# One list schedule for all engines' orders, and PSUM banks held in common, in an attention and MoE kernel

## The chip, the cores and the metric

The kernel runs on one core of a Trainium2 chip. The metric is the device time of one execution in microseconds (us). Five engines matter here: TensorE (PE, with its weight loads on a row of their own, PEld), VectorE (DVE), ScalarE (ACT), GpSimd (POOL) and SyncE (SP), which issues every DMA of this kernel. Each engine runs its own instructions strictly in the order in which the program holds them; an instruction that waits for a semaphore holds up everything behind it on its engine.

## The reference

Attention over 8 batches of 8 heads (576 positions, head size 64), in which scores more than tau below the maximum of their row are masked out. Its result goes through a two-layer block with a gated activation.

```python
scores = scale * np.matmul(q, k.transpose(0, 1, 3, 2))
thresh = np.max(scores, axis=-1, keepdims=True) - tau
scores = np.where(scores >= thresh, scores, -1000000000.0)
scores = scores - np.max(scores, axis=-1, keepdims=True)
attn = np.exp(scores)
attn = attn / (np.sum(attn, axis=-1, keepdims=True) + 1e-09)
out = np.matmul(attn, v)
...
h = x @ w_in                       # x: 4608 x 512, w_in: 512 x 2048
g = h * (1.0 / (1.0 + np.exp(-h)))
return (g @ w_out)                 # w_out: 2048 x 512
```

## The kernel before

**Attention.** The work goes by visits, one for a pair of heads, and by score tiles of 128 rows by 576 columns. A visit of batches 1 to 7 has nine tiles: four of each head, and one that holds the last 64 rows of both. Batch 0 is cut in two: four "low" visits with the first 256 rows, which take another path (transposes on PE), then four "high" visits with the other 320 rows. A tile goes through this chain. `scores` (L411): PE multiplies, with the keys split into a high and a low part; four matmuls of 288 columns, eight in the tile shared by two heads. `soft1`: DVE takes the row maximum (L421) and the threshold (L424). `soft1b`: ACT takes the exponential (L431). `soft2`: DVE masks and sums (L440), and takes the reciprocal (L444, L448). `soft2b`: ACT divides (L453). `soft3`: POOL makes a high part in half precision (L464; for the first tiles ACT does, L462) and two low parts (L467, L470), and SP issues a DMA that transposes them into `wT` (L480). After the last tile of a visit, `av` multiplies by the values (28 matmuls, L495), for two halves of the columns in batches 1 to 7; `av_post` splits the result into a high and a low part, `x16` (L513 on ACT, L514 on DVE). Two PSUM tiles hold scores, `x16` has two buffers, so that two batches can be under way.

**MoE.** When the last `av` of a batch half is through, that half gives 32 units: 16 of `h_unit` (12 matmuls, L529; then tanh on ACT L537, a product on DVE L538, the high part on ACT L546 and the low part on DVE L552, into `gbuf`), and 16 of `o_unit` (12 matmuls each, L567; four to an output tile, which ACT scales, L576, and SP stores, L578). There are 512 units in all, 64 to a batch.

**Preparing.** Queries and keys are loaded for each head (L290, L291) and split (L314, L315, L323, L325). The values are loaded for each pair (`vraw`, L232), their maximum is taken (L238), and a power of two for the batch (`vscale`, L110 to L136) scales their split (L275, L276). The 32 chunks of the weights come as 64-bit words and are decoded in the first part of the run by POOL, DVE, ACT and PE (L178 to L204), and split after that (L210, L211).

**What sets the order.** The program is written tile by tile: at step t come the softmax pieces of tile t, the scores of tile t+1, the last pieces of tile t-1, and what `at` planned for t; a `credit`, filled at a rate worked out for each batch half, says how many MoE units follow. Out of that the framework's scheduler, which runs a model of the engines, makes the order of each engine; `pri` raises chosen pieces by an offset (`PRI_S`, `PRI_SOFT1`, `PRI_SOFT2`). Of the eight PSUM banks four belong to the two score tiles, one to `av` (`ps_a`), and two, later three (`turn`), to everything else, taken in turn.

Of the kernel before, what the change touches and what calls it, by code (L numbers as in the profile page):

```python
# [19 lines left out]
P = 128  # L20
# [19 lines left out]
PRI_S, PRI_SOFT1, PRI_SOFT2 = 500, 50, 200  # L40

# [10 lines left out]
def attention_moe(  # L52
# [32 lines left out]

# [8 lines left out]


# [9 lines left out]
    def pow2_scales(mx, name, across=True):  # L105


        k = name[0]
        one = const.tile([P, 1], F32, name=f"{name}_one", tag=f"{k}_one")
        nc.vector.tensor_reduce(out=one, in_=mx, op=ALU.max, axis=AX.X)  # L110
        if across:


            diag = const.tile([P, P], BF16, name=f"{name}_diag", tag="diag")
            nc.scalar.activation(diag, ident, AF.Copy, scale=one)
            allp = bank([P, P], f"{name}_ps")
            nc.tensor.matmul(allp, ones, diag, start=True, stop=True)
            one = const.tile([P, 1], F32, name=f"{name}_all", tag=f"{k}_all")
            nc.vector.tensor_reduce(out=one, in_=allp, op=ALU.max, axis=AX.X)
        cl = const.tile([P, 1], F32, name=f"{name}_cl", tag=f"{k}_cl")  # L120
        nc.vector.tensor_scalar(
            out=cl, in0=one, scalar1=2.0**-20, scalar2=2.0**47, op0=ALU.max, op1=ALU.min
        )
        e2 = const.tile([P, 2], I32, name=f"{name}_e2", tag=f"{k}_e2")
        nc.vector.tensor_scalar(
            out=e2[:, 0:1], in0=cl.bitcast(I32), scalar1=EXPMASK, scalar2=None, op0=ALU.bitwise_and
        )
        nc.vector.tensor_scalar(
            out=e2[:, 1:2], in0=cl.bitcast(I32), scalar1=EXPMASK, scalar2=EXPMASK,
            op0=ALU.bitwise_and, op1=ALU.bitwise_xor,  # L130
        )
        sc = const.tile([P, 2], F32, name=f"{name}_sc", tag=f"{k}_sc", bufs=3)
        nc.vector.tensor_scalar(
            out=sc[:, 0:1], in0=e2[:, 1:2].bitcast(F32), scalar1=2.0**12, scalar2=None, op0=ALU.mult
        )
        nc.vector.tensor_scalar(  # L136
            out=sc[:, 1:2], in0=e2[:, 0:1].bitcast(F32), scalar1=2.0**-13, scalar2=None, op0=ALU.mult
        )
        return sc
# [6 lines left out]
    ones = const.tile([P, P], BF16, name="ones")  # L146
    nc.vector.memset(ones, 1.0)
    ident = const.tile([P, P], F32, name="ident")
    make_identity(nc, ident)
    wsc = {}  # L150

    w_words = (w_in.bitcast(I32), w_out.bitcast(I32))
    wraw = {}
    wps = {}

    def load_weights(i):
        if i < 4 * NK and i % 8 < 4:
# [12 lines left out]

    def decode_weights(i):


        t = wraw.pop(i)
        low, top = t[:, :, 0], t[:, :, 1]
        w = wst[:, i + WSPARE, :]
        wbits = w.bitcast(I32)
        nc.gpsimd.tensor_scalar(  # L178
            out=w, in0=top.bitcast(F32), scalar1=2.0**-112, scalar2=1.0,
            op0=ALU.mult, op1=ALU.mult,  # L180
        )
        nc.vector.tensor_scalar(
            out=wbits, in0=wbits, scalar1=3, scalar2=None, op0=ALU.logical_shift_left
        )
        nc.vector.scalar_tensor_tensor(  # L185
            out=wbits, in0=low, scalar=29, in1=wbits,
            op0=ALU.logical_shift_right, op1=ALU.bitwise_or,
        )


        n, c = divmod(i, 4)
        if c == 0:
            wps[n] = bank([P, P], f"wps_{n}", 2)
        upper = w.bitcast(BF16).rearrange("p (c t) -> p c t", t=2)[:, :, 1]
        for j in range(4):
            nc.tensor.matmul(
# [589 lines left out]
```

## Time and profile before

| what | value |
|---|---|
| timed runs | 1278.84, 1283.26, 1284.72 us; median 1283.26 us |
| span of the profiled execution | 1282.6 us; no other time of this execution is listed |
| TensorE clock granted, mean | 0.974 |
| instructions | 26842 |
| PE busy | 1164.2 us, 91% |
| DVE busy | 1001.3 us, 78% |
| ACT busy | 819.3 us, 64% |
| POOL busy | 794.6 us, 62% |
| DMA, packets' time as a share of 16 engines | 58.8%, 158.15 MB |

The page of the profile gives the busy time of each engine, then the span in 40 slices, then the DMA queues, the chain of work that ended last, and the groups of instructions by line. Other views of the trace give the same by stretches of time (busy time, granted clock and DMA share in each), by group with the idle time ahead of it, by who waited for whom, or instruction by instruction. A row of the groups reads: line, engine, operation, output and input, shape, count, then busy time in us and mean length of one in ns, then the idle time ahead of them and what ended it. The times of the three runs and the span agree within 0.3%.

### The profile page before, as it was taken

The page shows a single profiled execution, that of the slowest core. Times are in us where ns is not written, and L with a number is a line of the kernel's source. Part 1 is how long each engine was busy: PE and PEld are TensorE (multiplying, and loading weights), DVE is VectorE, ACT ScalarE, POOL GpSimd, SP SyncE. Part 2 cuts the span into 40 slices and gives each one's busy share as a digit, 9 for nine tenths or more (in the row PEclk, how much of TensorE's full clock was granted, in tenths as well). Part 3 has the DMA queues.
Part 4 walks back from the last instruction along what each step waited for, and adds up shares of the span by engine and source line. Part 5 has one row for each costly group of instructions (what it writes and reads, how often), then busy time and mean ns, then how long its engine had stood idle before and what let it go on. Part 6 is the DMA issues. An engine that isn't in the chain of part 4 may idle for free.

```text
span 1282.6 us, 26842 instructions
## 1 busy us (share of the span) xinstructions
PE 1164.2 (91%) x9400; PEld 891.7 (70%) x9400; DVE 1001.3 (78%) x2627; ACT 819.3 (64%) x1501; POOL 794.6 (62%) x956
## 2 busy tenths in 40 slices
PE   5675778799699989999999999999899999999998
PEld 3454546576577767777777777777677777877777
DVE  7999998987898978869795978868795979771431
ACT  5887767675777756757575757666575757661431
POOL 4559978676778657767665666776575766761000
PEclk8987899899999989999999999999999999999999
DMA  9456767868868557656755665657566655543000
GB/s 294 129 176 166 184 121 134 151 122 155 152 126 162 105 132 135 122 117 130 148 107 122 114 151 120 126 112 147 118 110 117 121 117 109 100 84 57 6 15 19
DMA packets 363479, 158.15 MB, mean 123 GB/s; under 512 B 329552, under 2 KB 338256, under 8 KB 363344
## 3 DMA queue, kind: packets, MB, share of 16 engines
q1 hardware_dynamic: 363344, 156.43, 58.8%
q8 instruction: 74, 1.21, 0.4%
q14 instruction: 61, 0.50, 0.1%
HBM read 66.72 MB, written 9.44 MB: 59 GB/s over the span
## 4 chain that ended last, share of the span: by engine, by line
PE 45%; DVE 26%; issue 8%; POOL 8%; DMA 7%; ACT 5%; SPq 1%; POOLq 0%; ACTq 0%; DVEq 0%
PE o L567 18%; PE h L529 14%; PE s L411 7%; PE a L495 6%; DVE w L440 5%; DVE sm L421 4%; DVE gbuf L552 4%; DMA wT<-hl 3%; POOL hl L467 3%; DVE qstack L315 2%; DMA vraw<-in_vL 2%; POOL hl L464 2%; DVE th L538 2%; POOL hl L470 2%; DVE wst L185 1%
## 5 line engine op out<-in xcount | busy, mean ns | idle before, releaser
L529 PE MATMUL h<-x,wst 128*128 128x288 f16 (+2 forms) x3072 | 417.2, 289 | 18.0 <-DVE th L538 16.3
L567 PE MATMUL o<-gbuf,wst 128*128 128x288 f16 (+2 forms) x3072 | 403.2, 287 | 8.2 <-DVE wst L211 5.8
L464 POOL TENSOR_SCALAR hl<-w 128x576 f16<-128x576 f32 x264 | 186.3, 706 | 294.1 <-ACT w L453 76.8
L529 PEld LDWEIGHTS <-wst 128*128 128x128 f16 x3072 | 290.5, 99 | 111.8 <-issue 31.2
L567 PEld LDWEIGHTS <-wst 128*128 128x128 f16 x3072 | 289.5, 98 | 95.4 <-DVE wst L211 9.2
L467 POOL TENSOR_TENSOR hl<-w,hl 128x512 f16<-128x512 f32 x272 | 338.3, 1244 | 12.4
L453 ACT ACTIVATE w<-w,sm 128x576 f32<-128x576 f32 x288 | 216.3, 769 | 109.4 <-DVE sm L448 103.6
L431 ACT ACTIVATE w<-s,sm 128x576 f32<-128x576 f32 x288 | 209.4, 735 | 117.6 <-POOL hl L470 74.8
L440 DVE SCALAR_TENSOR_TENSOR w<-s,sm,w 128x576 f32<-128x576 f32 x288 | 231.6, 811 | 64.8 <-ACT w L431 62.5
L421 DVE TENSOR_REDUCE sm<-s 128x1 f32<-128x576 f32 x288 | 214.7, 748 | 46.8 <-PE s L411 42.5
L411 PE MATMUL s<-khi,qstack 128*128 128x288 f32 x608 | 157.9, 342 | 42.6 <-DVE w L440 27.7
L552 DVE SCALAR_TENSOR_TENSOR gbuf<-th,gbuf 128x288 f16<-128x288 f32 (+2 forms) x256 | 158.6, 622 | 22.8 <-ACT gbuf L546 22.0
L495 PE MATMUL a<-wT,v 128*64 128x288 f16 (+1 forms) x1680 | 147.9, 302 | 8.4 <-DMA wT<-hl 6.8
L537 ACT ACTIVATE th<-h,msc 128x288 f32<-128x288 f32 (+2 forms) x256 | 126.1, 495 | 41.0 <-DVE gbuf L552 24.5
L411 PEld LDWEIGHTS s<-khi,qstack 128*128 128x128 f32 x608 | 96.1, 194 | 69.9 <-issue 52.0
L546 ACT ACTIVATE gbuf<-th 128x288 f16<-128x288 f32 (+2 forms) x252 | 110.0, 439 | 53.2 <-DVE th L538 52.7
L538 DVE SCALAR_TENSOR_TENSOR th<-th,h 128x288 f32<-128x288 f32 (+2 forms) x256 | 113.4, 445 | 30.7 <-ACT th L537 28.3
L411 PE MATMUL s<-klo,qstack 128*128 128x288 f32 x608 | 131.9, 299 | 0.0
L495 PEld LDWEIGHTS <-v 128*64 128x64 f16 x1680 | 94.7, 114 | 50.2 <-issue 39.5
L470 POOL TENSOR_TENSOR hl<-w,hl 128x64 f16<-128x64 f32 x272 | 122.0, 449 | 0.0
L325 POOL TENSOR_TENSOR klo<-kraw,khi 128x576 fp32r<-128x576 f32 x64 | 94.8, 1481 | 10.6 <-ACT khi L323 9.2
L411 PEld LDWEIGHTS s<-klo,qstack 128*128 128x128 f32 x608 | 99.9, 193 | 0.0
(85 smaller groups left out, 871.5 us busy)
## 6 DMA issues: line engine op xcount, KB each, us to landing
qraw<-in_qT SPq DMA_DIRECT2D x128, 144.0 KB, 3.0
kraw<-in_kT SPq DMA_DIRECT2D x128, 144.0 KB, 3.0
vraw<-in_vL SPq DMA_DIRECT2D x32, 320.0 KB, 3.6
wraw<-in_w_out SPq DMA_DIRECT2D x16, 512.0 KB, 3.9
out_t<-ot SPq DMA_DIRECT2D x56, 144.0 KB, 2.1
wT<-hl SPq DMA_TRANSPOSE x304, 3.3
gbuf<-in_w_in SPq DMA_DIRECT2D x8, 512.0 KB, 8.3
wraw<-in_w_in SPq DMA_DIRECT2D x8, 512.0 KB, 5.4
```

Source lines behind the costliest of these rows:

```text
L411: nc.tensor.matmul(s_ps[:, j, :HALF], lhs, kk[:, j * HALF : (j + 1) * HALF], start=(n == 0), stop=(n == len(seq) - 1),)
L421: nc.vector.tensor_reduce(out=negm, in_=s_ps[:, :, :HALF], op=ALU.max, axis=AX.XY, negate=True)
L431: nc.scalar.activation(wtile[t].rearrange("p (j c) -> p j c", j=2), sps[t][:, :, :HALF], AF.Exp, bias=small[t][:, 0:1],)
L440: nc.vector.scalar_tensor_tensor(out=w3, in0=s_ps[:, :, :HALF], scalar=sm[:, 1:2], in1=w3, op0=ALU.is_ge, op1=ALU.mult, accum_out=sm[:, 2:3],)
L453: nc.scalar.activation(w, w, AF.Copy, scale=r)
L464: nc.gpsimd.tensor_scalar(out=fl[:, 0:S], in0=w, scalar1=1.0, scalar2=1.0, op0=ALU.mult, op1=ALU.mult)
L467: nc.gpsimd.tensor_tensor(out=fl[:, 640:1152], in0=w[:, 0:512], in1=fl[:, 0:512], op=ALU.subtract)
L470: nc.gpsimd.tensor_tensor(out=fl[:, 576:640], in0=w[:, 512:576], in1=fl[:, 512:576], op=ALU.subtract)
L495: nc.tensor.matmul(a_ps[odd * D : (odd + 1) * D, :n], vt[:, lo_v, odd, kv, :], wT[v, b * H + 2 * p + odd][:, kw, c0 - base : c0 - base + n ...
L529: nc.tensor.matmul(ph[:, :n], wi(c, f, lo_w), x16[b, lo_x][:, c, c0 : c0 + n], start=(k == 0), stop=(k == 11),)
L552: nc.vector.scalar_tensor_tensor(out=g[:, 1, :n], in0=th[:, :n], scalar=2.0**-14, in1=g[:, 0, :n], op0=ALU.mult, op1=ALU.subtract,)
L567: nc.tensor.matmul(ps[:, :n], wo(f, d, lo_w), g[:, lo_g, :n], start=(f == 0 and k == 0), stop=(f == NF - 1 and k == 2),)
```

## The change

The kernel is written anew around a class `Plan`. Every piece of work becomes an operation with its engine, its occupancy and its latency in ns, a priority, the values it reads and writes, and what it needs from a pool. The pools stand for buffers: 2 score tiles, 4 banks in common for everything else, 3 `hl`, 3 `wT`, 17 `g`, and so on. `run` lays the operations out in time, while the program is being built: of the operations that are ready and find their buffers free it takes the one that can start first, and among those of one engine that can start by then the one with the smallest priority. `emit` then writes the instructions in the order of these starts, and the framework keeps that order. Semaphores between the engines are placed by the framework as before.

```diff
+class Plan:
+    def op(self, eng, occ, lat, prio, fn, reads=(), writes=(), part=False, hold=(), after=(), dma=None, name=""):
...
+    def run(self):
...
+        while len(done) < len(ops):
+            best = None
+            for e in engs:
+                es = [(t, o) for o in ready[e] for t in (est(o),) if t is not None]
+                if not es:
+                    continue
+                m = min(t for t, _ in es)
+                t, o = min((q for q in es if q[0] <= m), key=lambda q: (q[1].prio, q[1].idx))
+                if best is None or t < best[0]:
+                    best = (t, o)
...
+            o.start = t
+            ef[o.eng] = t + o.occ
+            o.end = t + o.lat
+            if o.dma is not None:
+                dma_free = max(t + 1000.0, dma_free) + o.dma
+                o.end = max(o.end, dma_free + 900.0)
...
+                    q.ready = max(d.end for d in q.deps) + SEM
...
-    ps_m = ctx.enter_context(tc.tile_pool(name="ps_m", bufs=1, space=PSUM))
-    ps_a = ctx.enter_context(tc.tile_pool(name="ps_a", bufs=1, space=PSUM))
+    ps_b = ctx.enter_context(tc.tile_pool(name="ps_b", bufs=1, space=PSUM))
...
+        ("s", 2), ("w32", 4), ("small", 4), ("hl", 3), ("wT", 3), ("qraw", 2), ("kraw", 2), ("khi", 2),
+        ("klo", 2), ("qst", 2), ("qz", 2), ("vraw", 5), ("v16", 4), ("x16", 2), ("th", 2), ("g", GB), ("ot", 2),
+    pl.pool("bank", 4, False)
...
+        op("PE", cost, cost + 100, u, lambda: score(s.t), reads, [s], name=f"score{nm}")
+        op("DVE", 670, 760, u, largest, [s], [mv], hold=[sm], name=f"max{nm}")
+        op("DVE", 125, 207, u, threshold, [mv], [tv], hold=[sm], name=f"thr{nm}")
+        op("ACT", 630, 740, u, exponential, [s, mv], [w], hold=[sm], name=f"exp{nm}")
+        op("DVE", 755, 890, u - 1, masked, [s, tv], [w, rv], hold=[sm], name=f"mask{nm}")
+        op("DVE", 140, 310, u - 1, reciprocal, [], [rv], hold=[sm], name=f"recip{nm}")
+        op("ACT", 660, 770, u - 1, divided, [rv], [w], hold=[sm], name=f"div{nm}")
...
+        if visits[v][0] == 0:
+            op("ACT", 610, 680, u - 1, lambda: high(True), [w], [hl], name=f"hi{nm}")
+        else:
+            op("POOL", 640, 710, u - 1, lambda: high(False), [w], [hl], name=f"hi{nm}")
+        op("POOL", 1400, 1600, u - 1, low, [w], [hl], name=f"lo{nm}")
...
+            op("PE", 1520 * k, 1620 * k, LATE + pr, unit, [x, *ws], [ph], hold=[X[b]], name=f"h{nm}")
+            op("ACT", 385 * k, 495 * k, URGENT + pr, tanh, [ph, scale], [th], name=f"tanh{nm}")
+            op("DVE", 366 * k, 445 * k, URGENT + pr, times, [ph], [th], name=f"times{nm}")
+            op("ACT", 334 * k, 440 * k, URGENT + pr, high, [th], [g], name=f"ghi{nm}")
+            op("DVE", 450 * k, 530 * k, URGENT + pr, low, [th], [g], name=f"glo{nm}")
...
+    pl.run()
+    with tc.manual_schedule():
+        pl.emit()
```

What is computed, the tiles and the operations stay the same, with two small moves: the high parts of all 20 tiles of batch 0's high visits are made on ACT (before, of the first 8), and those of the first four MoE units on ACT (before, on POOL). `LATE` puts the MoE products of PE behind all attention; `URGENT` puts what follows them on ACT and DVE ahead of everything. The priority of attention is the number of the tile, u.

Three places show what moves. The first is on DVE at the end of attention, where the last two `av` results of batch 7 are split (`a_7_3`, the rows that write `x16_7`); a row with `th_b_c_f` is the product that follows MoE unit f of batch b and the half that begins at column c. Before:

```order
L538 SCALAR_TENSOR_TENSOR th_6_288_15_16042<-th_6_288_15_16042,h_6_288_15_15995 128x288
L552 SCALAR_TENSOR_TENSOR gbuf_61<-th_6_288_15_16042,gbuf_61 128x288
L514 SCALAR_TENSOR_TENSOR x16_7_1_14793<-a_7_3_0_16273,x16_7_0_14792 128x288
L514 SCALAR_TENSOR_TENSOR x16_7_1_14793<-a_7_3_288_16319,x16_7_0_14792 128x288
L538 SCALAR_TENSOR_TENSOR th_7_0_0_16376<-th_7_0_0_16376,h_7_0_0_16350 128x288
L538 SCALAR_TENSOR_TENSOR th_7_0_1_16394<-th_7_0_1_16394,h_7_0_1_16363 128x288
```

And now:

```order
L757 SCALAR_TENSOR_TENSOR th_6_0_12_15534<-th_6_0_12_15534,h_6_0_12_15487 128x288
L765 SCALAR_TENSOR_TENSOR gbuf_61<-th_6_0_12_15534,gbuf_61 128x288
L710 SCALAR_TENSOR_TENSOR x16_7_1_14557<-a_7_3_0_15505,x16_7_0_14556 128x288
L710 SCALAR_TENSOR_TENSOR x16_7_1_14557<-a_7_3_288_15540,x16_7_0_14556 128x288
L757 SCALAR_TENSOR_TENSOR th_6_0_13_15599<-th_6_0_13_15599,h_6_0_13_15571 128x288
```

The end of attention has moved from behind both halves of batch 6 to the thirteenth unit of batch 6's first half. On PE, where the same place lies between the same units, 115 of the 512 MoE units stand behind the last `av` now, and 64 did before, but for the first two that are cut in pieces around it.

The second place is on DVE at the first `av` result of batch 4 (`a_4_0_0`, the row that writes `x16_4`); rows with `w32` are the masks of score tiles. Before:

```order
L538 SCALAR_TENSOR_TENSOR th_3_0_7_8441<-th_3_0_7_8441,h_3_0_7_8391 128x288
L552 SCALAR_TENSOR_TENSOR gbuf_61<-th_3_0_6_8404,gbuf_61 128x288
L444 TENSOR_SCALAR sm_174_8799<-sm_174_8799 128x1
L440 SCALAR_TENSOR_TENSOR w32_175_8853,sm_175_8852<-s_175_8803,sm_175_8852,w32_175_8853 128x576
L514 SCALAR_TENSOR_TENSOR x16_4_1_8497<-a_4_0_0_8449,x16_4_0_8496 128x288
```

And now:

```order
L757 SCALAR_TENSOR_TENSOR th_2_288_15_8180<-th_2_288_15_8180,h_2_288_15_8152 128x288
L574 SCALAR_TENSOR_TENSOR w32_21b0_8171,sm_21b0_8149<-s_21b0_8116,sm_21b0_8149,w32_21b0_8171 128x576
L765 SCALAR_TENSOR_TENSOR gbuf_61<-th_2_288_15_8180,gbuf_61 128x288
L710 SCALAR_TENSOR_TENSOR x16_4_1_8188<-a_4_0_0_8186,x16_4_0_8187 128x288
```

When batch 4 delivers its first result, MoE is at the end of the `h` units of batch 2's second half; before, it was eight units into batch 3. By the PE rows, 176 units stand ahead of this place now, and 196 before.

The third place is on DVE where the maxima of batch 2's values are taken (rows that write `vmx_2`, from `vraw_2_1` to `vraw_2_3`). Before:

```order
L238 TENSOR_REDUCE vmx_2_2286<-vraw_2_1_2373 128x1
L315 SCALAR_TENSOR_TENSOR qstack0_85<-qraw_10_12_2748,gate_79,qstack0_85 64x576
L440 SCALAR_TENSOR_TENSOR w32_61_2655,sm_61_2654<-s_61_2584,sm_61_2654,w32_61_2655 128x576
L238 TENSOR_REDUCE vmx_2_2286<-vraw_2_2_2778 128x1
L424 TENSOR_SCALAR sm_62_2732<-sm_62_2732,ntau_81 128x1
L514 SCALAR_TENSOR_TENSOR x16_1_1_2692<-a_1_0_0_2620,x16_1_0_2691 128x288
L238 TENSOR_REDUCE vmx_2_2286<-vraw_2_3_3189 128x1
```

And now:

```order
L443 TENSOR_REDUCE vmx_2_110<-vraw_2_2_1996 128x1
L580 TENSOR_SCALAR sm_9a2_2494<-sm_9a2_2494 128x1
L583 RECIPROCAL sm_9a2_2494<-sm_9a2_2494 128x1
L560 TENSOR_REDUCE sm_9a3_2550<-s_9a3_2527 128x1
L560 TENSOR_REDUCE sm_9a4_2590<-s_9a4_2535 128x1
L563 TENSOR_SCALAR sm_9a3_2550<-sm_9a3_2550,ntau_78 128x1
L443 TENSOR_REDUCE vmx_2_110<-vraw_2_3_2016 128x1
```

The three maxima stood within seven rows around the first result of batch 1. Now the first of them stands some sixty rows further ahead, and the loads of the last two are issued by SP among the transposes of visits 7 and 8, where before they came among those of visits 8 and 9.

More of the change, by code (lines that the diff above doesn't have):

```diff
@@ L191, in decode_weights @@
         n, c = divmod(i, 4)
         if c == 0:
[L193 to L196, printed above, removed]
-                wps[n], ones, upper[:, j * P : (j + 1) * P],
-                start=(c == 0 and j == 0), stop=(c == 3 and j == 3),
-            )
-        if c == 3:
-            nc.vector.tensor_reduce(out=wmx[:, n : n + 1], in_=wps[n], op=ALU.max, axis=AX.X)
-        sg = stage.tile([P, 512], F16, tag="wsg", name=f"wsg_{i}", bufs=2)
@@ new lines, in weight_chunk, with summed, signs @@
+        ps = WREAD[n]
+        def summed():
+            upper = w.bitcast(BF16).rearrange("p (c t) -> p c t", t=2)[:, :, 1]
+            for j in range(4):
+                nc.tensor.matmul(
+                    ps.t[:, 0:P], ones, upper[:, j * P : (j + 1) * P],
+                    start=(c == 0 and j == 0), stop=(c == 3 and j == 3),
+                )
+        sg = tiled("wsg", [P, 512], F16, f"wsg_{i}", 2, stage)
+        def signs():
+            nc.scalar.activation(sg.t, raw.t[:, :, 1].bitcast(F32), AF.Sign)
@@ L294, in qcol, with prepare_qk, load @@
     def qcol(h, i):
         return i * P if h % 2 == 0 else (0, 384, 512, 128, 256)[(i + 1) % 5]
-    def split_q(h, tiles):
-        qr = qkraw[h][0]
+    def prepare_qk(v, h, tiles, u):
+        b, hh = divmod(h, H)
         odd = h % 2
+        qr = tiled("qraw", [P, S], F32, f"qraw_{v}_{h}", 2)
+        kr = tiled("kraw", [P, S], F32, f"kraw_{v}_{h}", 2)
+        kh = tiled("khi", [P, S], F32R, f"khi_{v}_{h}", 2)
+        kl = tiled("klo", [P, S], F32R, f"klo_{v}_{h}", 2)
+        qs = pl.value(f"qs_{v}_{h}", "qst")
+        for x, src in ((kr, kT), (qr, qT)):
+            for r in range(2):
+                def load(x=x, src=src, r=r):
+                    nc.sync.dma_start(out=x.t[r * D : (r + 1) * D, :], in_=src[b, hh])
+                op("SP", 600, 3000, u - 7, load, [], [x], part=True, dma=620, name=f"load_qk{h}")
@@ L350, in soft3_direct, with khigh, klow @@
-    def soft3_direct(t):
-        w = wtile.pop(t)
-        v, parts = tiles[t]
-        base, n = VISITS[visits[v][2]][2][0]
-        main = bank([P, 4, P], f"tm_{t}")
-        for k in range(4):
-            nc.tensor.transpose(main[:, k, :], w[:, k * P : (k + 1) * P], ident)
-        last = bank([P, P], f"tl_{t}")
-        nc.tensor.transpose(last, w[:, S - P : S], ident)
+        def khigh():
+            nc.scalar.activation(kh.t, kr.t, AF.Copy)
+        def klow():
+            nc.gpsimd.tensor_tensor(out=kl.t, in0=kr.t, in1=kh.t.bitcast(F32), op=ALU.subtract)
@@ L605, in attention_moe, with visit, tile_of, score @@
+    def visit(v, b, p, kind, u):
         ta, tb, ranges = VISITS[kind]
-        u = len(tiles)
-        start.setdefault((b, p), u)
         ha = b * H + 2 * p
+        qk = {}
+        def tile_of(h, i, nm, parts, heads, u):
+            seq = [(hh, kk) for hh in heads for kk in (1, 2)]
+            def score(s):
+                for m, (hh, kk) in enumerate(seq):
+                    c = qcol(hh, i)
+                    for j in range(2):
+                        nc.tensor.matmul(
+                            s[:, j, :HALF], qstack[hh % 2][:, c : c + P],
+                            qk[hh][kk].t[:, j * HALF : (j + 1) * HALF],
+                            start=(m == 0), stop=(m == len(seq) - 1),
+                        )
+            reads = [x for hh in heads for x in qk[hh]]
+            softmax(nm, u, v, parts, score, reads, 540 * len(heads), False)
+        qk[ha] = prepare_qk(v, ha, ta, u)
```

1050 lines of the change are left out of this document (548 added, 502 removed).

## The prediction

> **What bounds the kernel now.** I began with the page's slices and cut the span where PE begins the first `av` of each batch (0 to 7), then behind the last one. The view of stretches gives for each: length, then busy time of PE, PEld, DVE, ACT and POOL, granted clock, DMA share, GB/s.
>
> ```profile
> 0.00:113.50 113.50, 73.79 (x405) 50.75 (x406) 100.98 (x239) 82.82 (x153) 65.47 (x73) 0.88 0.66 196
> 113.50:222.40 108.90, 83.46 (x634) 60.94 (x634) 104.07 (x248) 78.47 (x136) 93.53 (x104) 0.94 0.67 146
> 222.40:339.80 117.40, 99.55 (x763) 73.32 (x762) 98.06 (x263) 76.68 (x133) 84.39 (x105) 0.94 0.76 143
> 339.80:493.90 154.10, 144.68 (x1188) 113.04 (x1187) 130.02 (x358) 105.91 (x191) 108.76 (x137) 0.98 0.71 137
> 493.90:636.60 142.70, 136.91 (x1156) 106.19 (x1157) 116.54 (x315) 93.76 (x173) 95.03 (x117) 1.00 0.63 126
> 636.60:778.70 142.10, 136.90 (x1156) 106.21 (x1157) 114.87 (x315) 93.71 (x174) 95.86 (x117) 1.00 0.62 127
> 778.70:924.50 145.80, 138.49 (x1156) 107.17 (x1157) 116.79 (x315) 93.61 (x173) 94.25 (x115) 0.99 0.61 120
> 924.50:1060.30 135.80, 133.31 (x1130) 103.53 (x1129) 109.95 (x303) 89.75 (x166) 91.77 (x112) 1.00 0.63 120
> 1060.30:1187.00 126.70, 124.86 (x1078) 97.15 (x1078) 80.47 (x216) 70.14 (x134) 65.55 (x84) 1.00 0.46 85
> 1187.00:1282.60 95.60, 92.23 (x753) 73.43 (x752) 29.55 (x65) 34.45 (x73) 0.00 (x0) 0.99 0.04 13
> ```
>
> Up to 222.4 us DVE is the bound: 100.98 + 104.07 = 205.1 us busy, 92% of the time, while PE lacks work. From 339.8 us on PE is nearly always busy, but busy is not work: ends are modelled. So I priced PE by starts, in the chain and the timeline of PE.
>
> ```profile
> 1185.16 1.84 PE a L495 x28
> 1208.67 23.52 PE o L567 x192
> 1255.71 23.53 PE o L567 x192
> ```
>
> ```profile
> 845.44 0.52 PE L411 MATMUL s<-khi,qstack 128*128 128x288 f32 x2
> ...
> 846.60 1.28 PE L529 MATMUL h<-x,wst 128*128 128x288 f16 x9
> 847.62 0.52 PE L411 MATMUL s<-khi,qstack 128*128 128x288 f32 x2
> ...
> 848.25 2.50 PE L529 MATMUL h<-x,wst 128*128 128x288 f16 x19
> ```
>
> 192 matmuls in 23.52 us make a MoE unit of 12 cost 1.47 us. An `av` costs 1.84 us. A score tile costs 848.25 - 847.62 = 0.63 us, the tile of two heads 846.60 - 845.44 = 1.16 us. A full batch is then 64 x 1.47 = 94.1, plus 32 x 0.63 + 4 x 1.16 = 24.8, plus 8 x 1.84 = 14.7: 133.6 us. The stretch from 493.9 us does that work in 142.7 us, so PE yields **0.936** of its time. In the stretch from 1060.3 us the order holds 62 units, 26 score tiles' worth and 8 `av`: 91.1 + 16.4 + 14.7 = 122.2 of 126.7 us, 0.965. What is left behind the last `av`, 64 units, runs without a gap (64 x 1.47 = 94.1 of 95.6 us). So PE loses at least 65 us up to 222.4 us (busy 157.3), some 29 in the next stretch (33 units and 39.5 us of attention make 88 of 117.4), and some 50 in the six behind it.
>
> One rule speaks about the way of reading itself. The page's PE row says 91%; taken as work, it leaves 1282.6 - 1164.2 = 118 us, all in gaps. The Trainium skill (Trainium Kernel Development and Optimization, Performance Expectations) calls matmul busy time a bad metric for the distance to the roofline, because matmuls are pipelined. The trace agrees: 136.9 us busy hold 133.6 us of starts. By busy time the forecast below would have a floor of 1164 + 65 + 18 (the gaps of the first three stretches) + 3 = 1250 us; by starts it has not.
>
> **The change part by part.** No work goes away; only orders move. DVE has the same content ahead of batch 1's first `av` in both orders (50 tile maxima, 32 decoded and 32 split weight chunks, 16 or 18 MoE units; 452 and 455 rows). Behind it, the PE order spreads MoE otherwise. Units between the first `av`s of batches 1, 2, 3, 4, 5, 6, 7 and the last `av`: 43, 50, 51, 65, 64, 64, 28 now, against 33, 64, 64, 64, 64, 63, 62 before; 115 behind it against 64. Attention runs ahead, MoE fills, and the end is a long stretch of MoE alone, the one kind of stretch that PE does without loss.
>
> The terms, stretch by stretch, each as the larger of PE's price over a yield and DVE's busy time over a share. I take 0.95 for PE, between the 0.936 and 0.965 above, and 0.92 for DVE, what it reaches up to 222.4 us. DVE's content beyond a row's own is priced with these groups.
>
> ```profile
> L538 DVE SCALAR_TENSOR_TENSOR th<-th,h 128x288 f32<-128x288 f32 (+2 forms) x256 | 113.4, 445 | 30.7 <-ACT th L537 28.3
> L552 DVE SCALAR_TENSOR_TENSOR gbuf<-th,gbuf 128x288 f16<-128x288 f32 (+2 forms) x256 | 158.6, 622 | 22.8 <-ACT gbuf L546 22.0
> L238 DVE TENSOR_REDUCE vmx<-vraw 128x1 f32<-128x640 f32 x32 | 26.0, 814 | 25.8 <-DMA vraw<-in_vL 25.6
> L464 POOL TENSOR_SCALAR hl<-w 128x576 f16<-128x576 f32 x264 | 186.3, 706 | 294.1 <-ACT w L453 76.8
> L467 POOL TENSOR_TENSOR hl<-w,hl 128x512 f16<-128x512 f32 x272 | 338.3, 1244 | 12.4
> L470 POOL TENSOR_TENSOR hl<-w,hl 128x64 f16<-128x64 f32 x272 | 122.0, 449 | 0.0
> ```
>
> 1. To batch 1: 205.1 us of DVE. At 0.92 it would stay 222.4. Of the 17 us idle about 7 are the first loads; half of the rest may go: **217** (bounds 212 and 226).
> 2. Batch 1 to 2: DVE 98.1 us plus 3.5 `h` units more at 445 + 622 ns, 101.8; over 0.92, **110** (117.4 before, in which DVE waits for late loads, the L238 row). PE needs 43 x 1.47 + 39.5 = 102.7, and is hidden.
> 3. Batch 2 to 3: PE 73.5 + 43 score tiles' worth at 0.62 (26.7) + 14.7 = 114.9; over 0.95, **121** (154.1 before).
> 4. Batch 3 to 4: the DVE content of the stretch from 493.9 us, 36 tiles and 32 `h`, 116.5 us; over 0.92, **127** (142.7). PE: 114.5 / 0.95 = 120.5.
> 5. Batch 4 to 5: PE 95.6 + 46 x 0.62 + 14.7 = 138.8; over 0.95, **146**.
> 6. and 7. Full batches, 133.6 / 0.95 = **140.6** each.
> 8. To the last `av`: 41.2 + 16 x 0.63 + 14.7 = 66.0; over 0.95, **69.5**.
> 9. 115 units at 1.47 = 169.1, and from the last matmul's end (1255.71 + 23.53 = 1279.24) to the span's end 3.4: **172.5**.
>
> The sum is 217 + 110 + 121 + 127 + 146 + 281.2 + 69.5 + 172.5 = **1244 us**. It is a span, set against the span of 1282.6; the median of the runs is 0.7 us above that.
>
> Smaller edits. For the common banks I looked at who waits on PE.
>
> ```profile
> PE s L411 <- DVE w L440: 27.7, 22, 4.3
> PE h L529 <- DVE th L538: 16.3, 17, 3.1
> PE a L495 <- DVE x L514: 1.6, 2, 1.3
> DVE vmx L238 <- DMA vraw<-in_vL: 25.6, 17, 3.6
> ```
>
> An `h` unit waited 16.3 us in all for a bank to be read; with four for all it can gain those 16.3 or, where an `av` finds none, lose about the 1.6 us that it waits now. I take nothing beside the yield, in which it lies. Twelve high parts more on ACT cost 12 x 0.7 = 8 us there, between 113.5 and 222.4 us, where ACT is busy 78.5 of 108.9 us; they free as much on POOL (93.5 busy), which is fuller. Cover: DVE, 104 us busy; without it ACT would still have room. SP's one queue now holds the `vraw` loads some tiles earlier, past transposes that wait for POOL; DVE's 25.6 us may go, or as much may come back where a load of keys stands behind a blocked transpose: -25.6 to +25.6 on DVE, and on PE little, since DVE is not the bound from stretch 5 on. I count only the 7 us in stretch 2. The third place in the change, the maxima of batch 2, is where this would show.
>
> **The rivals.** *Better:* the orders fit so well that PE yields 0.98 and DVE 0.96. For it: PE's idle time in full batches is only 5.8 of 142.7 us now and comes from orders laid by other lengths. Against: three engines are fuller at once (DVE at 0.92). 213.6 + 106 + 117 + 121 + 141.6 + 272.6 + 67.3 + 172.5 = 1212 us.
>
> *Given back:* PE yields 0.92 and DVE 0.90, because scores stand at fixed places between whole units of 12 matmuls, and PE waits at each that comes late (27.7 us now). 222.4 + 113 + 125 + 129.5 + 151 + 290 + 72 + 172.5 = 1276 us, at the border of no change.
>
> *Slower, by lengths that are too short:* the table counts 640 + 1400 = 2040 ns of POOL for a tile; the rows above add up to 706 + 1244 + 449 = 2399. That is 0.36 us short for each of 36 tiles, 13 us a batch. If every batch's attention comes that much later than its places in the PE order, the 5.5 batches up to the last `av` cost 71 us: 1316 us. It decides from 3.5 such batches on (38.6 + 6.4 us over the forecast). Against: POOL needs 36 x 2.4, and 8 times the 1.4 us of the L325 row below, 98 us in a stretch of 121 to 146, so it can catch up. What makes POOL long is visible where both engines meet:
>
> ```profile
> 671.55 1.40 POOL L325 TENSOR_TENSOR klo<-kraw,khi 128x576 fp32r<-128x576 f32 x1
> ...
> 671.63 1.62 DVE L552 SCALAR_TENSOR_TENSOR gbuf<-th,gbuf 128x288 f16<-128x288 f32 x1
> ```
>
> The DVE operation began 0.08 us behind POOL's and ended 0.3 us after it, 1.62 us long where the group's mean is 0.622. The Trainium skill (SBUF — State Buffer, Who interferes with whom) states that a DVE instruction with two SBUF inputs and a GpSimd instruction that reads SBUF lock each other out for a whole instruction. This trace agrees. By that rule the meetings grow with POOL's load, 95 of 142.7 us now and about 98 of 124 in stretches 3 and 4; without it the lengths would stay.
>
> *Not what it says:* that the orders barely differ is excluded by the rows shown.
>
> **How the numbers follow.** Forecast, 1225 to 1262 around 1244: 0.46. Better, 1212: 0.25. Given back, 1276: 0.15, on both sides of the border. Slower, 1316: 0.14. A difference of 0.5% is about what a measurement of this kernel can tell from none: faster means below 1276, slower above 1289. Faster: 0.46 + 0.25 + 0.04 = 0.75; same 0.11; slower 0.14. The range goes from 1203 (the better case with PE at 0.99 and stretch 1 at its 212) to 1290, behind the case of gains given back; it leaves out the worst case and a small part below.
>
> **What would show it.** Right: first `av` of batch 2 before 335 us; stretches 3 and 4 of about 120 us with DVE over 90% busy; last `av` near 1070 us; 172 us of MoE alone. Wrong: PE waiting ahead of scores at many places in stretches 3 to 7 (given back), POOL without idle time there and PE idle together (slower), or a first `av` of batch 1 later than 226 us, which would say that the start's order has become worse.

## The result, and the profile after

The changed kernel takes **1269.32 us** (median of 4 runs, 1268.0 to 1271.38). The kernel before takes 1283.99 us beside it (4 runs, 1278.84 to 1285.76, a spread of 0.5%). The ratio is **0.989**, with a 95% interval of 0.986 to 0.991: faster, by 1.1%, where 3% was forecast. The profiled execution has a span of 1268.3 us, and its granted clock is 0.960 over the span.

These are the stretches of the changed kernel, cut where PE begins the first `av` of each batch and behind the last one. The columns are those of the prediction's first fence: length, then busy time of PE, PEld, DVE, ACT and POOL, granted clock, DMA share, GB/s.

```profile
0.00:233.00 233.00, 156.02 (x1010) 116.54 (x1010) 215.45 (x495) 172.24 (x306) 155.83 (x164) 0.81 0.67 171
233.00:351.80 118.80, 110.39 (x895) 84.60 (x894) 110.69 (x304) 86.87 (x155) 91.64 (x115) 0.96 0.77 148
351.80:481.60 129.80, 116.72 (x998) 93.66 (x997) 121.55 (x313) 90.90 (x161) 96.23 (x120) 0.99 0.74 142
481.60:606.20 124.60, 116.23 (x1002) 92.92 (x1001) 116.87 (x315) 93.81 (x172) 99.89 (x123) 1.00 0.75 148
606.20:751.80 145.60, 138.99 (x1190) 112.05 (x1189) 132.31 (x359) 106.48 (x190) 101.18 (x126) 1.00 0.71 133
751.80:890.30 138.50, 133.54 (x1157) 107.61 (x1155) 116.34 (x313) 96.44 (x174) 93.87 (x116) 1.00 0.65 128
890.30:1029.50 139.20, 133.48 (x1153) 107.60 (x1152) 114.91 (x300) 95.24 (x173) 91.97 (x116) 1.00 0.67 120
1029.50:1095.70 66.20, 65.59 (x626) 53.53 (x626) 46.87 (x126) 40.07 (x73) 46.32 (x62) 1.00 0.66 111
1095.70:1268.30 172.60, 169.20 (x1382) 134.92 (x1380) 47.56 (x105) 56.55 (x121) 0.00 (x0) 1.00 0.05 15
```

Beside the nine terms of the forecast:

| stretch | 1 | 2 | 3 | 4 | 5 | 6 | 7 | 8 | 9 |
|---|---|---|---|---|---|---|---|---|---|
| forecast | 217 | 110 | 121 | 127 | 146 | 140.6 | 140.6 | 69.5 | 172.5 |
| measured | 233.0 | 118.8 | 129.8 | 124.6 | 145.6 | 138.5 | 139.2 | 66.2 | 172.6 |

The first three came out 33.6 us longer than forecast, the other six together 9.5 shorter. In the first four, DVE is busy for 92.5, 93.2, 93.6 and 93.8% of the time: by that share it is the bound for the first 606 us, where it was for 222 before; in the fourth stretch PE is nearly as busy (93.3%). The chain that ended last says the same. First its shares by engine before, then after:

```profile
PE 45%; DVE 26%; issue 8%; POOL 8%; DMA 7%; ACT 5%; SPq 1%; POOLq 0%; ACTq 0%; DVEq 0%
```

```profile
DVE 45%; PE 38%; issue 7%; ACT 4%; DMA 3%; POOL 2%; SPq 1%; ACTq 0%; POOLq 0%; DVEq 0%
```

DVE's groups that answer to those shown of before (L765 is the old L552, L757 the old L538, L443 the old L238):

```profile
L765 DVE SCALAR_TENSOR_TENSOR gbuf<-th,gbuf 128x288 f16<-128x288 f32 (+2 forms) x256 | 163.9, 642 | 46.7 <-ACT gbuf L762 45.9
L757 DVE SCALAR_TENSOR_TENSOR th<-th,h 128x288 f32<-128x288 f32 (+2 forms) x256 | 114.6, 448 | 77.4 <-ACT th L754 73.7
...
L443 DVE TENSOR_REDUCE vmx<-vraw 128x1 f32<-128x640 f32 x32 | 25.9, 810 | 10.6 <-DMA vraw<-in_vL 10.4
```

The wait for late loads of values fell from 25.6 to 10.4 us, as hoped; the low part of `g` became 20 ns longer. How the middle loses time is seen in PE's timeline within stretch 3; the bracket holds PE's idle time ahead of the row and what ended it. These are rows with a wait alone:

```profile
409.34 0.50 PE L866 MATMUL s_15a<-khi,qstack 128*128 128x288 f32 x2 [0.36 <-DVE w_15a L574]
...
425.56 0.51 PE L866 MATMUL s_15b<-khi,qstack 128*128 128x288 f32 x2 [1.83 <-DVE w_15b L574]
...
433.96 0.50 PE L866 MATMUL s_16a<-khi,qstack 128*128 128x288 f32 x2 [1.02 <-DVE w_15b L574]
...
437.87 0.50 PE L866 MATMUL s_16a<-khi,qstack 128*128 128x288 f32 x2 [0.18 <-DVE w_15b L574]
```

Each of these waits stands ahead of a score tile, and DVE's mask of an earlier tile (L574), which frees a score bank, ends it. PE's order is fixed, so the MoE units behind the score wait too. So DVE is later than the places that PE's order leaves for it; that its lengths in the table are the reason is what the experiments ask.

For the comparison of experiments I divide a span in three: the **start** (to batch 2's first `av`), the **middle** (to batch 7's first `av`) and the **end**. In the changed kernel they take 351.8, 677.7 and 238.8 us and hold 75, 294 and 143 MoE units. I take the prices of the prediction (1.47 us a unit, 1.84 an `av`, 0.63 a score tile, 1.16 a tile of two heads). For what PE does in the start for the low visits and the weights I take 41.5 us in every run, an estimate from the spacing of those matmuls. By them PE loses 128.8, 41.4 and 3.9 us in the three parts; in the kernel before the same count gives 130.2, 50.4 and 7.7. The prices are those of a full clock. The granted clock of the start is 0.86 in the changed kernel and 0.92 before, so its loss holds some of that too.

### The profile page after: what moved, and what is told of

The parts are those of the page before. It is cut to its first block, busy times and chain, and to the rows that moved or that the text cites. A ratio compares the mean times of both kernels' runs of the same rounds, so it can differ in the third digit from the quotient of the medians.

```text
span 1268.3 us, 26945 instructions
## 1 busy us (share of the span) xinstructions
PE 1140.2 (90%) x9400; PEld 903.4 (71%) x9400; DVE 1022.5 (81%) x2627; ACT 838.6 (66%) x1517; POOL 776.9 (61%) x940
## 4 chain that ended last, share of the span: by engine, by line
DVE 45%; PE 38%; issue 7%; ACT 4%; DMA 3%; POOL 2%; SPq 1%; ACTq 0%; POOLq 0%; DVEq 0%
PE o L784 15%; PE h L747 13%; DVE gbuf L765 7%; PE a L698 4%; DVE th L757 4%; DVE qstack L533 3%; DVE wst L409 2%; DVE v L463 2%; DVE wst L357 1%; DVE wst L354 1%; DMA vraw<-in_vL 1%; PE a L690 1%; DVE x L710 1%; DVE vmx L443 1%; DMA qraw<-in_qT 1%
## 5 line engine op out<-in xcount | busy, mean ns | idle before, releaser
L765 DVE SCALAR_TENSOR_TENSOR gbuf<-th,gbuf 128x288 f16<-128x288 f32 (+2 forms) x256 | 163.9, 642 | 46.7 <-ACT gbuf L762 45.9
L757 DVE SCALAR_TENSOR_TENSOR th<-th,h 128x288 f32<-128x288 f32 (+2 forms) x256 | 114.6, 448 | 77.4 <-ACT th L754 73.7
L698 PE MATMUL a<-wT,v 128*64 128x288 f16 (+1 forms) x1680 | 113.7, 294 | 0.0
L698 PEld LDWEIGHTS <-v 128*64 128x64 f16 x1680 | 94.5, 112 | 16.3 <-issue 6.5
L795 ACT ACTIVATE ot<-o,msc 128x288 f32<-128x288 f32 (+2 forms) x64 | 31.6, 494 | 87.2 <-PE o L784 85.6
L533 DVE SCALAR_TENSOR_TENSOR qstack<-qraw,gate,qstack 64x576 fp32r<-64x576 f32 x56 | 63.3, 1131 | 4.4 <-ACT qstack L525 2.6
L381 POOL TENSOR_TENSOR wst<-wst,wsg 128x512 f32<-128x512 f32 x32 | 40.5, 1272 | 34.3 <-PE wps L370 14.2
L513 ACT ACTIVATE khi<-kraw 128x576 fp32r<-128x576 f32 x64 | 43.2, 674 | 0.0
L525 ACT ACTIVATE qstack<-qraw,gate 128x576 fp32r<-128x576 f32 x56 | 43.0, 769 | 0.0
L463 DVE SCALAR_TENSOR_TENSOR v<-vraw,v_s,v 128x640 f16<-128x640 f32 x32 | 38.7, 1213 | 0.5 <-ACT v L460 0.5
L844 PE MATMUL s_d<-kd,gbuf 128*128 128x288 f32 x64 | 24.4, 520 | 14.6 <-DVE w_d L574 8.3
L710 DVE SCALAR_TENSOR_TENSOR x<-a,x 128x288 f16<-128x288 f32 (+1 forms) x60 | 27.0, 452 | 12.0 <-ACT x L705 11.8
L705 ACT ACTIVATE x<-a 128x288 f16<-128x288 f32 (+1 forms) x60 | 23.9, 403 | 17.2 <-PE a L698 17.0
L443 DVE TENSOR_REDUCE vmx<-vraw 128x1 f32<-128x640 f32 x32 | 25.9, 810 | 10.6 <-DMA vraw<-in_vL 10.4
```

What stands on the lines that cost most here:

```text
L463: nc.vector.scalar_tensor_tensor(out=o.t[:, 1], in0=raw.t, scalar=VS[b].t[:, 0:1], in1=o.t[:, 0], op0=ALU.mult, op1=ALU.subtract)
L513: nc.scalar.activation(kh.t, kr.t, AF.Copy)
L525: nc.scalar.activation(dst, qr.t[:, c0:c1], AF.Copy, scale=gate)
L533: nc.vector.scalar_tensor_tensor(out=dst[D:P, :], in0=qr.t[D:P, c0:c1], scalar=gate[D:P, :], in1=dst[D:P, :].bitcast(F32), op0=ALU.mult, o ...
L698: nc.tensor.matmul(a.t[odd * D : (odd + 1) * D, :n], vt.t[:, lo_v, odd, kv, :], w2[odd].t[:, kw, c0 - base : c0 - base + n], start=(k == 0 ...
L757: nc.vector.scalar_tensor_tensor(out=th.t[:, :n], in0=th.t[:, :n], scalar=1.0, in1=ph.t[:, :n], op0=ALU.add, op1=ALU.mult)
```

## The experiments

Two theories stood at first: that DVE is slower than its lengths in the table, because POOL and DVE lock each other out, and that the pair of small operations behind each mask (guard and reciprocal, one operation of the plan) costs more than the 140 ns it is charged. The rival for the pair was that standing next to each other is the cost itself. All ratios are to the kernel before on the same chip, with 95% intervals.

**1. Separate banks for `av`.**

```diff
-    pl.pool("bank", 4, False)
+    pl.pool("bank", 3, False)
+    pl.pool("abank", 1, False)
```

> The changed kernel with its list schedule, but the four common PSUM banks divided again: three for everything, one for av alone. Tells the part of the common banks from the part of the order. Theory (DVE is the bound of the first 480 us, PE behind that, so banks matter little): within 6 us of the changed kernel's 1269, h units' waits for a bank under 10 us. Rival (the gain over the kernel before is the banks'): back to 1280 or more, and PE waiting for DVE L757 by 15 us or more.

1263.83 us, ratio 0.983 (0.980 to 0.986). Common banks bring nothing that shows: with a bank of its own for `av`, an `h` unit waits 3.9 us in all for a bank (7 times). Whether the 5 us less are an effect was asked of a control.

**2. Control: the same plan with a neutral constant changed.** `SEM` is what the planner adds to a value's end for a semaphore. Six ns more redraw many ties of the order and mean nothing else.

```diff
-SEM = 60
+SEM = 66
```

> A control: the changed kernel with the plan's time for a semaphore at 66 ns and not 60, which changes the order here and there and nothing else. It measures how far the time moves when the plan merely draws another order. Theory (the gains of the other edits are their own): 1269 within 8 us. Rival (any other order may bring 20 us or more): outside 1255 to 1283.

1263.65 us, 0.983 (0.981 to 0.986). This redrawn order differs by some 5 us, so a single edit of the plan that yields about 5 us is not told apart from chance. Experiment 1 is inconclusive within that; most of the gains below are far outside it. It is one draw alone, though, and experiment 10 may show one that costs more.

**3. The lock taken away at POOL, with the order untouched.**

```diff
-nc.gpsimd.tensor_tensor(out=fl[:, 640:1152], in0=w.t[:, 0:512], in1=fl[:, 0:512], op=ALU.subtract)
+nc.gpsimd.memset(fl[:, 640:1152], 0.0)
```

It leaves out 512 of the 576 columns of the low half of the attention weights. POOL then only writes there, and takes 524 ns for it.

> The changed kernel with the same plan and the same order, but POOL writes zeros into the first 512 columns of the low part of the attention weights and does not compute them: POOL's largest reader of SBUF is left out. Theory lock: the DVE operations with two SBUF operands come down toward their shortest lengths by more than half of their excess (106 us over the whole run, some 55 of them in the first 482 us), so the first av of batch 4 comes 20 to 35 us earlier and the span is 1235 to 1250. Rival content (DVE's own work and its dependent pairs fill the time): these operations shorten little, the span stays above 1262.

1210.32 us, 0.941 (0.938 to 0.945). The groups of DVE in this run, same columns as above:

```profile
L765 DVE SCALAR_TENSOR_TENSOR gbuf<-th,gbuf 128x288 f16<-128x288 f32 (+2 forms) x256 | 130.7, 512 | 48.7 <-ACT gbuf L762 47.6
L757 DVE SCALAR_TENSOR_TENSOR th<-th,h 128x288 f32<-128x288 f32 (+2 forms) x256 | 115.2, 450 | 79.3 <-ACT th L754 75.6
```

And its first three stretches:

```profile
0.00:217.80 217.80, 154.85 (x1014) 117.27 (x1016) 197.46 (x496) 170.46 (x306) 127.95 (x165) 0.81 0.73 184
217.80:330.40 112.60, 107.61 (x898) 83.83 (x894) 105.42 (x307) 88.15 (x158) 64.50 (x117) 0.97 0.84 156
330.40:447.30 116.90, 113.20 (x1001) 92.74 (x997) 108.27 (x310) 89.44 (x159) 66.19 (x119) 1.00 0.83 156
```

L765, which reads two SBUF operands, falls from 642 to 512 ns; L757, which reads one of its two from PSUM, stays at 450. In the start DVE is busy 23.3 us less (326.1 to 302.9), and the start is 21.4 us shorter: it follows DVE nearly one to one. The granted clock of stretch 1 is 0.81 with and without this edit (0.88 and 0.94 in that part before), so these 21 us are not the clock's. Nor can PE's lower clock have cost the changed kernel much there: DVE waits for PE for some 4 us in its whole start. The middle goes from 677.7 to 642.6 us with the same order and units. At 1210 us the gain is larger than either expectation, and this run alone doesn't separate DVE's lengths from POOL's own, which fell as well.

**4. The lock taken away at DVE.** The product (1 + tanh)·h goes back into its PSUM bank, so that the operation that makes `g`'s low part has one SBUF operand; POOL's work stays.

```diff
-out=th.t[:, :n], in0=th.t[:, :n], scalar=1.0, in1=ph.t[:, :n], op0=ALU.add, op1=ALU.mult
+out=ph.t[:, :n], in0=th.t[:, :n], scalar=1.0, in1=ph.t[:, :n], op0=ALU.add, op1=ALU.mult
...
-out=g.t[:, 1, :n], in0=th.t[:, :n], scalar=2.0**-14, in1=g.t[:, 0, :n],
+out=g.t[:, 1, :n], in0=ph.t[:, :n], scalar=2.0**-14, in1=g.t[:, 0, :n],
```

> The changed kernel, but the product (1 + tanh) * h is written back into its PSUM bank, so that the DVE operation that makes the low part of g reads one operand from PSUM and one from SBUF, not two from SBUF. Theory lock (two-operand SBUF reads on DVE wait for POOL's instructions): its mean length falls from 642 ns to about 460; some 80 of 256 lie in the first 482 us, where DVE is the bound: 80 x 0.18 = 15 us, 1255. Rival (the first 482 us are bound by a chain of waits between engines and not by DVE's work): the length may fall, the time stays at 1269 within 4 us; if the lengths stay, the lock is not what makes them long.

1222.84 us, 0.952 (0.948 to 0.955). In its groups and its third to fifth stretch:

```profile
L765 DVE SCALAR_TENSOR_TENSOR gbuf<-h,gbuf 128x288 f16<-128x288 f32 (+2 forms) x256 | 115.3, 454 | 40.6 <-ACT gbuf L762 39.7
```

```profile
347.00:463.10 116.10, 114.67 (x1005) 93.36 (x1003) 108.43 (x311) 89.18 (x158) 92.47 (x118) 1.00 0.79 151
463.10:575.70 112.60, 111.41 (x989) 90.86 (x987) 105.18 (x301) 88.37 (x165) 90.63 (x118) 1.00 0.88 159
575.70:713.20 137.50, 135.78 (x1181) 111.29 (x1179) 124.46 (x358) 104.79 (x190) 104.11 (x133) 1.00 0.76 147
```

L765 takes 454 ns, 188 less, about its length in the table (450); 256 of them make 48 us of DVE. The expectation had 15 us, from the first 482 us; the span is 49.5 us shorter, 44.8 of them in the middle. The middle falls from 677.7 to 632.9 us, which is PE's price (the loss is -2.6 by these prices, so none): PE is the bound there. The plan has other dependencies by this edit and so another order as well. In the start it brings only 4.8 us. A meeting like the one in the prediction, in this run:

```profile
692.36 1.17 POOL L640 TENSOR_TENSOR hl_25a<-w_25a,hl_25a 128x512 f16<-128x512 f32 x1
...
692.65 0.46 DVE L765 SCALAR_TENSOR_TENSOR gbuf<-h,gbuf 128x288 f16<-128x288 f32 x1
```

DVE's operation runs through while POOL's is under way. The Trainium skill (SBUF — State Buffer, Who interferes with whom) says that a DVE instruction with at most one SBUF input, outside what it calls 2-port modes, does not contend with GpSimd, and that one with two SBUF inputs contends with a GpSimd instruction that reads SBUF, not with one that only writes it. The two runs agree with both halves: 454 ns with one SBUF input, and 512 ns in the mean where POOL's `memset` only writes.

The rival that PSUM is merely quicker to read than SBUF falls by the traces themselves. In the changed kernel, L765 with both operands in SBUF takes 455 ns in the mean where no POOL instruction runs beside it (124 of its instructions of 288 columns), and 1042 ns where it begins inside POOL's L640 (54). In experiment 3 it takes 462 ns where it begins inside the `memset` (27).

**5. The same edit in the kernel before**, with all high parts of `g` on ACT.

> The kernel before with the same edit as above: the product of tanh stays in its PSUM bank, and ACT makes all high parts of g. Theory (the lock costs DVE as much there, 256 x 0.17 = 43 us in all, but DVE is the bound only up to 222 us, where 16 of these operations lie, and PE behind that): 3 to 12 us, 1272 to 1280. Rival (the lock is what the change has made dear): no gain at all there, or a loss through the banks that are held longer, 1284 or more. Rival (DVE bounds the kernel before in every stretch): 1240 or less.

1281.34 us, 0.998 (0.995 to 1.000). L552 fell there from 622 to 451 ns, 44 us of DVE, and the time by 2. The start gained 15.6 us (339.8 to 324.2), and the middle gave back 11.5 (720.6 to 732.1), in an order that the scheduler laid anew. In the middle DVE was busy for 588 of 720.5 us before (82%), against 602 of 677.7 in the changed kernel (89%), so there was less for it to bound. The `h` bank is held longer by this edit, but that isn't what gave the time back: the waits of `h` units for a bank fell from 16.3 to 6.6 us. That the new order is what made DVE's length matter fits this; the redrawn order of this run is not separated from it.

**6. The pair as two operations of the plan**, so that other work can stand between.

```diff
-        op("DVE", 140, 310, u - 1, reciprocal, [], [rv], hold=[sm], name=f"recip{nm}")
+        op("DVE", 65, 145, u - 1, guarded, [], [rv], hold=[sm], name=f"guard{nm}")
+        op("DVE", 75, 160, u - 1, reciprocal, [], [rv], hold=[sm], name=f"recip{nm}")
```

> The changed kernel, but the addition and the reciprocal of a tile are two operations of the plan and not one. In the changed kernel all 288 pairs stand next to each other on DVE, the second begins 34 ns behind the end of the first, where independent neighbours overlap by 82 ns: 0.116 us lost each. Theory pairs (DVE bounds the first 482 us and each pair costs it 0.116 us there): some 150 tiles lie there, at least 80% of the pairs come apart, 13 us gained, 1256. Rival (DVE has room, its busy share of 93% means waits): unchanged within 4 us, 1269.

1240.85 us, 0.966 (0.963 to 0.968). Of 288 adjacent pairs 46 are left. What a pair takes is seen in DVE's timeline of the changed kernel:

```profile
566.90 0.15 DVE L580 TENSOR_SCALAR sm_20a<-sm_20a 128x1 f32<-128x1 f32 x1
567.09 0.16 DVE L583 RECIPROCAL sm_20a<-sm_20a 128x1 f32<-128x1 f32 x1
567.17 0.14 DVE L580 TENSOR_SCALAR sm_20a<-sm_20a 128x1 f32<-128x1 f32 x1
```

The reciprocal starts 0.19 us behind the guard that it reads, 0.04 after its end. The next tile's guard, which reads nothing of it, starts 0.08 behind the reciprocal, inside it. This pair holds DVE for 567.17 - 566.90 = 0.27 us, and 0.26 is the median of all 288; the table has 0.14. That is 36 x 0.12 = some 4.3 us a batch. In the kernel before, 74 of the 288 pairs stood next to each other like this; the plan's one operation made it all of them. The gain of 28 us is twice the expected 13. Two explanations are left by this run: the gap itself, or the wrong length.

**7. The pair left together and charged what it takes.**

```diff
-        op("DVE", 140, 310, u - 1, reciprocal, [], [rv], hold=[sm], name=f"recip{nm}")
+        op("DVE", 260, 340, u - 1, reciprocal, [], [rv], hold=[sm], name=f"recip{nm}")
```

> The changed kernel, but the plan charges a tile's reciprocal pair what it takes (260 ns on DVE, 340 to its end, for 140 and 310); both instructions stay next to each other. Theory pairs (the 0.116 us lost at each pair is the cost): little, 1262 to 1271. Rival lengths (the plan's wrong length puts everything behind it at wrong places, and the 28 us of the split came from a truer table): 1240 to 1250.

1241.17 us, 0.966 (0.964 to 0.969): the same as split. The instructions and the gap are all there; the number, with the order that follows from it, brought 28 us. For the time as a whole the theory that adjacency is the cost has fallen, and the short length in the table is it. The middle went from 677.7 to 651.2 us at 293 units, PE's loss there from 41.4 to 16.3. The start alone is 348.5 us here and 344.1 with the pair split, as that theory would have it; the middle is 651.2 and 656.1, the other way round.

**8. The same, charged 120 ns too much** (380 and 460).

> The changed kernel with the reciprocal pair charged at 380 ns, 120 more than it takes, as the change charged 120 less. Theory (truth of the table counts: too long is wrong as well, but an engine that is ahead of the plan only waits a little): within 8 us of the true table's 1241. Rival (slack on DVE is what helps, whatever the truth): better than 1233. Rival (only the exact value helps, and 1241 was a lucky order): back to 1255 or more.

1237.57 us, 0.964 (0.961 to 0.966). Too long costs nothing in all: the middle's loss falls further, to 8.3 us, and the start grows from 348.5 to 354.4 us. Three plans that no longer charge the pair too little, each with its own order, lie within 4 us of each other (1240.85, 1241.17, 1237.57), so their gain is hardly chance.

**9. Other lengths made true, the pair left at 140**: POOL's two operations of a tile 690 and 1660 ns (640 and 1400), the low parts of `g` 555 (450), of decoded weights 1050 (850) and of values 1050 (950).

> The changed kernel with other entries of its table at the mean lengths of the trace: POOL's high part 690 and low parts 1660 ns (640 and 1400 before), the low part of g on DVE 555 (450), the splits of the weights and of the values on DVE 1050 (850 and 950). The reciprocal pair stays at 140 for 260. Theory (any entry of DVE that is too short lets DVE fall behind the plan, and PE stands at its fixed places): the entries mended here make DVE 32 x 0.1 = 3.4 us a batch longer, as the pair's 36 x 0.12 = 4.3 did, so a similar gain: 1240 to 1252. Rival (it is POOL's entries, 12.9 us a batch short, that were dear): 1225 to 1240. Rival (only the pair mattered): 1260 to 1270.

1248.13 us, 0.971 (0.968 to 0.974). The middle takes 658.8 us, its loss is 23.9. These entries were worth 21 us and the pair 28. Whether the two add up was not run. The middle's losses that they take away (17.5 and 25.1 us) would together be all of its 41.4. How much is POOL's and how much DVE's share of this edit was not separated.

**10. Both splits (pair, and the two steps of decoding a weight) and PSUM together.**

> Both edits together in the changed kernel: the pairs of a tile's reciprocal (and those of the weights' decoding, shift and join) are separate operations of the plan, and the product of tanh stays in its PSUM bank. Theory (DVE's work in the first 480 us is what the time hangs on, and the two take different parts of it): the gains add up as far as DVE is the bound, 46 + 28 = 74 us at most, less what PE takes over as the bound: 1205 to 1215. Rival (each gain is only another draw of the order): no better than the better of the two, 1222.

1234.43 us, 0.960 (0.958 to 0.963), worse than PSUM alone and than either expectation. Its plan draws another start: 61 MoE units ahead of batch 2's first `av` instead of 75 to 77, and a loss of 133.4 us there. In the middle nothing is lost (1.1 us). Why the planner chose so was not followed up. If it is chance, a draw can cost more than the control's 5 us: here 11.6 against PSUM alone.

**11. PSUM, and the pair charged 260.**

> The product of tanh in its PSUM bank and the reciprocal pair charged at its true 260 ns, in the changed kernel. Theory (what costs is that DVE falls behind the plan; the first edit alone already took the loss of PE behind batch 2 to nothing): at most a few us beyond the first edit's 1223, 1212 to 1224. Rival (each takes its own share): 1195 to 1205.

**1210.0 us**, 0.942 (0.939 to 0.945), 1206.31 to 1212.26 in 4 runs: the best that computes all, ahead of both kernels. It takes 337.2, 632.5 and 237.9 us in the three parts. Nearly all that it wins over PSUM alone lies in the start (347.0 to 337.2), where plans differ by as much without such an edit, so how much of it is the pair's is open.

**12. The same, with the decoding of weights due earlier.**

```diff
-W_AT = (4.0, 16.0)
-W_STEP = 1.0
+W_AT = (3.0, 13.0)
+W_STEP = 0.8
```

> As the kernel with the product in PSUM and the true pair, but the weights are planned earlier, as in the kernel before: the two groups from tile 3 and 13 in steps of 0.8 (4 and 16, 1.0). Theory (the start is bound by DVE's whole work up to batch 1, whatever its order): first av of batch 1 within 4 us of the kernel without this. Rival (the late second group delays the o units and leaves PE without work): first av of batch 1 6 us earlier or more MoE ahead of it, and the time 6 to 12 us lower.

1212.23 us, 0.944 (0.941 to 0.946): no difference. Start 340.1 us, again with 75 units: when the weights are due is not what holds it. That DVE's work as a whole does is the theory's other half; the table of the starts, in the next section, bears on it.

## Why the prediction was too good

The direction and the range (1203 to 1290) held; the gain was 14.3 us of span instead of 38.6. Step by step:

- **Attention ahead, MoE alone at the end: right.** Stretch 9 took 172.6 us, forecast 172.5. Batch 2's `av` did not begin before 335 us but at 351.8; the last `av` came at 1095.7 where 1070 was named.
- **Terms 1 and 2: the step that failed.** It read "DVE has the same content ahead of batch 1's first `av` in both orders", and kept 205.1 us; for stretch 2 it added 3.5 units to 98.1. The content was compared by the count of a few kinds. Measured, DVE was busy 215.5 + 110.7 = 326.1 us where 306.9 were counted: 19.2 us of the 25 by which the start was missed. The other 5.6 are idle time of DVE in stretch 1, which stayed (17.5 us, 17.3 before) where term 1 left 12. Batch 1's first `av` came at 233.0 us, past the 226 that the prediction named as the sign of a worse start.
- **What the start held more.** The sum of the lengths of DVE's instructions up to batch 2's first `av` grew from 354.7 to 375.2 us. Nearly all of that is count at the old means: eight more low parts of `g`, six more products, more tiles begun, more of the values' scales; the forecast had 3.7 us of it, its 3.5 units. The lengths moved both ways and about cancel: L409 (the low halves of the decoded weights) is 159 ns longer for its 32, L354 187 shorter. In stretch 1 the sum grew by 4.6 us only and the busy time by 10.4, because DVE's instructions run into each other less (30.0 us of overlap, 35.8 before): all its 48 reciprocal pairs stand together there, and 5 did before; 43 more at 0.10 us are some 4 us of it, an estimate. "No work goes away; only orders move" put that at nothing. The share of busy time was right (0.927). The waits for loads hardly fell in the start (9.4 to 8.0 us); they fell behind it.
- **Terms 3 to 7: right in sum (675.2 forecast, 677.7 measured), not in their reasons.** Term 3 took PE as the bound; DVE was, with 121.55 us busy of 129.8. Term 4 did take DVE, 127 us, and measured 124.6. What I put down as a yield of 0.95 is mostly DVE behind its table: with one length mended the loss falls from 41.4 to 16.3 us, with L765's lock gone to none. So this sum hid a fault that could be mended, and 1244 is met by the kernel with the true length (1241.17) through a shorter middle than forecast (651.2) and a longer start (348.5).
- **"Slower, by lengths that are too short"** named the right mechanism. It put it on POOL alone (0.36 us a tile); the entries of DVE were short too, and the price was smaller than its 71 us: all that PE lost in the middle was 41.4. POOL was not without idle time: 483 of 677.7 us busy in the middle. Its meetings with L765 are little of what makes POOL long: with that operand in PSUM, its three operations of a tile take 2287 ns in the mean, and 2349 without.
- **"Given back"** foresaw PE waiting ahead of scores at fixed places. The timeline above shows it. Its sum of 1276 was near, though its start (335.4 us) was too short and its middle (695.5) too long.
- **"Better"**, 1212 us, is where the kernel comes with both faults gone (1210.0), with a longer start than that rival's (337.2 against 319.6) and a shorter middle (632.5 against 652.2).
- **Lock growth counted at nothing: partly wrong.** The L765 group grew by 5.3 us in all (158.6 to 163.9). What mattered was that the lock was never in the table: 450 ns there, 642 on the chip.
- **Common banks at nothing: not refuted**; the run with a bank of its own for `av` lies within the control's scatter.

The start follows DVE's busy time in every plan, at nearly one share:

| run | start, us | DVE busy, us | share |
|---|---|---|---|
| changed kernel | 351.8 | 326.1 | 0.927 |
| 3, POOL's reads left out | 330.4 | 302.9 | 0.917 |
| 4, PSUM | 347.0 | 321.8 | 0.927 |
| 6, pair split | 344.1 | 320.6 | 0.932 |
| 7, pair charged 260 | 348.5 | 326.9 | 0.938 |
| 8, pair charged 380 | 354.4 | 329.8 | 0.931 |
| 11, PSUM and 260 | 337.2 | 315.0 | 0.934 |
| 12, weights earlier | 340.1 | 312.2 | 0.918 |

So PE's loss in the start, 119.8 us in experiment 6 and 129.1 in experiment 8 at 76 and 77 units, differs by DVE's work: 9.2 us more busy in the second. Against the kernel before the loss is the same (128.8 and 130.2 us). Open: which choices of the planner put how much of DVE's work ahead of batch 2's first `av`, and what would shorten the idle time that is left there (some 25 us).

## What to carry to other kernels

A static order is as good as the lengths it was laid by on the engine that bounds: two dependent instructions in one operation need the time they hold the engine for, and an entry that is too long was far cheaper here than one that is too short (one entry, 120 ns either way). Before pricing a moved order, sum every instruction that stands ahead of the cut on the bound engine, not the kinds that come to mind. An intermediate that VectorE reads again can stay in PSUM, where GpSimd's reads didn't hold it up; it brought 46 us in the order in which VectorE came late, and 2 in the order before.

## What was not expected of the hardware

A DVE instruction of 128x1 that reads its neighbour's result starts 0.18 us behind its start in the median of 288 pairs, and what follows the pair starts 0.08 behind the second one: over 288 tiles that is 288 x 0.10 = 29 us of DVE. And the lock reaches far: taking one of two SBUF operands away shortened 256 instructions by 188 ns each, and leaving out POOL's reads shortened L463 from 1213 to 1034 ns and L409 on the first layer's weights from 1342 to 1010.

```profile
L463 DVE SCALAR_TENSOR_TENSOR v<-vraw,v_s,v 128x640 f16<-128x640 f32 x32 | 33.0, 1034 | 0.5 <-ACT v L460 0.5
...
L409 DVE SCALAR_TENSOR_TENSOR wst<-wst,i_w_s 128x512 f16<-128x512 f32 x16 | 16.1, 1010 | 0.0
```
